# Twenty-eight float16 warm-up matmuls become three in float32 (linear attention followed by a silu MLP)

## The chip, the cores and the metric

The kernel runs on one core of one Trainium2 chip. The metric is the device time of one execution in microseconds. Five engines take part: TensorE (PE, with its weight loads listed apart as PEld), VectorE (DVE), ScalarE (ACT), GpSimd (POOL) and SyncE (SP), the last of which only issues DMA transfers here.

## The reference

For each of 8 batches and 8 heads, with 576 rows and 64 columns, the kernel computes an attention without a score matrix, and runs its result through a two-layer MLP:

```python
q_s = softmax(q, axis=-1)            # over the 64 columns
k_s = softmax(k, axis=2)             # over the 576 rows
kv  = einsum('bhsd,bhse->bhde', k_s, v)
x   = einsum('bhsd,bhde->bhse', q_s, kv)   # heads side by side: 4608 x 512
h   = x @ w_in                       # 512 x 2048
out = (h * sigmoid(h)) @ w_out       # 2048 x 512, float32
```

The warm-up matmuls compute nothing of this. They multiply a tile of zeros, and what they write to PSUM is overwritten before anything reads it.

## The kernel before

The order of all work is written out by hand. `ORDER` is a long list of names. Each name stands for a closure in `ops`, and the last loop of the kernel calls them in that order. Every engine works through its own instructions in that order; semaphores hold an instruction until what it reads is there. Nothing is moved by a planner, so taking a name out of the list moves nothing else.

The head of the list treats batch 0 alone, and it is this part that the change touches:

- SP loads q, k and v of batch 0 in two halves (`lq0.*`, `lk0.*`, `lv0.*`, line 152). A half `c` has four heads. Meanwhile DVE clears the tile `warm` (line 546) and converts the identity matrix (line 559), and TensorE starts on `heat0`.
- For each half: ACT takes exp(q) (`eq0.*`, line 163), DVE sums it and takes the reciprocal (`z0.*`, lines 207 to 211) and scales (`n0.*`, line 216), TensorE transposes the scaled q into PSUM (`tr0.*`, line 234, nine blocks of 128 columns), and ACT and DVE copy the transposes to SBUF (`tc0.*`, lines 142 and 144).
- For each half, beside that: ACT takes exp(k) (`ek0.*`, line 168), v is cast (`vc0.*`, on ACT for half 0, on ACT and DVE for half 1), TensorE forms kv with a column of ones for the softmax sum (`kv0.*`, line 248, 36 small matmuls of 64 by 64 by 65), and DVE divides by that sum (`kc0.*`, lines 259 and 261).
- Then `X0.*` (line 282) multiplies the transposed q by kv, and ACT and DVE bring the product to SBUF (`x0.*`).
- After `X0.1` the wide first layer of batch 0 begins (`w0.0`, `w2.0` and so on, line 307): 128 matmuls of 288 columns. From there on the list gives TensorE one matrix product after another until the end: the second layer, and for the later token tiles two layers of products by a Strassen-like scheme (lines 425 and 503).

The weights come by DMAs issued from POOL in four pieces of `w_in` (`W1a0` and `W1a1`, `W1b`, `W1c`, `W1d`, line 567), then pieces of `w_out` (line 573). The piece `W1b` holds the weights from the fifth block of the first layer on.

Four groups of warm-up matmuls stand in this head, all from line 564 and each 128 by 128 by 512 in float16:

- `heat0`, 20 of them into PSUM bank 5, ahead of the first transposes `tr0.0`
- `heat1`, 5 into bank 5, between `tr0.0` and `kv0.0`
- `heat2`, 1 into bank 6, between `X0.0` and `kv0.1`
- `heat3`, 2 into bank 3, between `kv0.1` and `X0.1`

Their operand `warm` is a view of `XS4[0]`, a float16 tile that is used for something else only much later.

Of the kernel before, what the change touches and what calls it, by code (L numbers as in the profile page):

```python
# [8 lines left out]
FP32 = mybir.dt.float32  # L9
# [7 lines left out]

ORDER = """
    lq0.0 lq0.1 lk0.0 lv0.0 lk0.1 lv0.1 gate W1a0 W1a1 W1b W1c W1d heat0 eq0.0.0 z0.0.0 eq0.0.1 z0.0.1 eq0.1 lq1.0
    lq1.1 W2a n0.0 ek0.0 z0.1 tr0.0 vc0.0 heat1 n0.1 tc0.0b kv0.0 tc0.0a kc0.0 tr0.1 ek0.1 vc0.1b X0.0 heat2 tc0.1b  # L20
    vc0.1a kv0.1 kc0.1 tc0.1a x0.0v heat3 X0.1 x0.0a x0.1v w0.0 w2.0 w1.0 x0.1a W2b1 lk1.0 w1.1 h1 w0.1 w3.0 w2.1
    W2b2 w3.1 h0 v1 v0 w5.0 w5.1 w4.0 w4.1 h2 v2 h3 w6.0 w6.1 h5 v3 h4 v5 w7.0 w7.1 h7 WS1.1 w9.0 v4 h6 w9.1 WS0.1
    w8.0 w8.1 v7 lk1.1 h9 h8 w11.0 v6 eq1.0.0 w11.1 v9 v8 h11 WS1.2 w10.0 lv1.1 w10.1 v11 w12.0 w12.1 eq1.0.1 W2c1
    h10 w13.0 lv1.0 v10 w13.1 w15.0 h12 h13 qp1a w15.1 v12 qp1b h15 v13 w14.0 eq1.1.0 z1.0 w14.1 eq1.1.1 p0 WS0.3 p1
# [46 lines left out]
def kernel(  # L71
# [9 lines left out]
    nc = tc.nc  # L81
# [9 lines left out]
    TCH = 512  # L91
# [15 lines left out]
    mp = ctx.enter_context(tc.tile_pool(name="mp", bufs=2))  # L107
# [10 lines left out]
    XS4 = [glob.tile([128, 2, HT], FP16, name=f"XS{i + 1}") for i in range(4)]  # L118
# [7 lines left out]
    dummy = glob.tile([1, 1], FP32, name="dummy")  # L126
    PS = ps.tile([128, 8, 512], FP32, name="PS")

    warm = XS4[0].rearrange("p a n -> p (a n)")
    B11, B12 = W2[:, 0:HF, 0:HN], W2[:, 0:HF, HN:DM]  # L130
    B21, B22 = W2[:, HF:NFB, 0:HN], W2[:, HF:NFB, HN:DM]
    T3 = B12
# [426 lines left out]
    nc.vector.tensor_copy(ident, ident_f)  # L559
    nc.vector.memset(vaug[:, :, :, D:E1], 1.0 / XS)  # L560

    def heat(n, bank=5):
        for _ in range(n):
            nc.tensor.matmul(out=PS[:, bank, :], lhsT=warm[:, 0:128], rhs=warm, start=True, stop=True)

    def load_w1(f0, f1, c0=0, c1=NC):
        nc.gpsimd.dma_start(
# [17 lines left out]
    def op(name, f, *args):  # L585
        assert name not in ops
        ops[name] = lambda: f(*args)
# [30 lines left out]
    for c, b0, b1 in ((0, 4, 0), (1, 6, 2)):  # L618
        op(f"X0.{c}", lambda c=c, b0=b0, b1=b1: (xt_mm(0, c, 0, 320, b0, 0), xt_mm(0, c, 320, 256, b1, 0)))
        op(f"x0.{c}a", xt_evac, 0, c, b0, 0, 320, 0, nc.scalar)  # L620
        op(f"x0.{c}v", xt_evac, 0, c, b1, 0, 256, 320, nc.vector)
    for i, (n, bank) in enumerate(((20, 5), (5, 5), (1, 6), (2, 3))):
        op(f"heat{i}", heat, n, bank)
    op("gate", lambda: nc.gpsimd.tensor_copy(gate, st[0]["kt", 0][0:1, 1, 0:1]))
    for x, f, n, c0, c1 in (("W1a0", 0, 4, 0, 2), ("W1a1", 0, 4, 2, 4), ("W1b", 4, 4, 0, 4), ("W1c", 8, 4, 0, 4), ("W1d", 12, 4, 0, 4)):
        op(x, load_w1, f, f + n, c0, c1)
# [38 lines left out]
    for b in range(1, B):  # L665
# [10 lines left out]
        if b > 1:  # L676
            bank = 2 if b in KV_WITH_X.values() else 6
# [16 lines left out]
    for t in range(1, NCH):  # L694
# [6 lines left out]
        for g in range(2):  # L701
            n = f"{t}.{g}."
# [123 lines left out]
```

## Time and profile before

| | us |
|---|---|
| median of three runs | 256.94 |
| lowest and highest of them | 256.66, 257.74 |
| the profiled execution, its own time | 256.38 |
| its span, from the first to the last instruction | 254.6 |
| TensorE busy in the span | 248.8 |
| VectorE busy | 207.0 |
| ScalarE busy | 190.7 |
| GpSimd busy | 66.0 |

All numbers of an execution's inside come from the profiled one. It lies 0.56 us under the median, and 1.8 us of its time lie outside the span. Times on the timeline count from the span's start. A row of the timeline gives the start, the length, the engine, the line, the operation, what is written and read, its size, how many instructions are merged into the row, and in brackets how long the engine had been idle and what ended that. A matmul's record lasts until its result is out, so the records of successive matmuls overlap: the pace of a row of them is read from the starts, not from the length of one.

### The profile page before, as it was taken

The numbers are of one execution on the slowest core, as the hardware profiler recorded it, in microseconds if no ns is written. First come the engines' busy times: TensorE is split into PE (matmuls) and PEld (weight loads), VectorE is DVE, ScalarE is ACT, GpSimd is POOL, SyncE is SP. The second block draws the span as 40 slices with busy tenths as digits, with TensorE's granted clock in tenths as the row PEclk, the third lists the DMA queues.
The fourth block names the chain that finished last, engine by engine and source line by source line (L and its number), as shares of the span: only waits on it lengthen the run. The fifth ranks groups of instructions, "written<-read, shape, count | busy, mean of one in ns | idle before, by whom it ended". The sixth has DMA issues, their size and how long they took to land.

```text
span 254.6 us, 6459 instructions
## 1 busy us (share of the span) xinstructions
PE 248.8 (98%) x2728; PEld 204.3 (80%) x2728; DVE 207.0 (81%) x277; ACT 190.7 (75%) x226; POOL 66.0 (26%) x62
## 2 busy tenths in 40 slices
PE   8899999999999999999999999999999999999994
PEld 2467746667888888888888888888888888888883
DVE  2969998899999989997998986996569836886752
ACT  4866867899999999999879889736597656674311
POOL 1753872730451540530082050006000000000022
PEclk9999999999999999999999999999999999999999
DMA  6999999799949939995955950030807000700355
GB/s 251 345 205 299 282 333 330 292 168 391 401 104 270 401 114 225 350 297 145 324 215 103 216 213 0 3 75 10 175 3 165 3 1 3 158 9 0 71 137 125
DMA packets 36238, 45.90 MB, mean 180 GB/s; under 512 B 16481, under 2 KB 21281, under 8 KB 36209
## 3 DMA queue, kind: packets, MB, share of 16 engines
q1 hardware_dynamic: 29408, 33.56, 45.4%
q0 software_dynamic: 6160, 11.60, 17.6%
q10 hardware_dynamic: 640, 0.33, 0.6%
q8 instruction: 21, 0.34, 0.5%
q14 instruction: 9, 0.07, 0.1%
HBM read 36.70 MB, written 9.44 MB: 181 GB/s over the span
## 4 chain that ended last, share of the span: by engine, by line
PE 81%; DMA 10%; ACT 3%; POOL 2%; DVE 2%; issue 1%; ACTq 0%
PE PS L503 37%; PE PS L425 34%; DMA qt<-in_q_dram 6%; PE PS L307 4%; DMA vt<-in_v_dram 3%; PE PS L335 2%; PE PS L282 2%; PE PS L248 2%; ACT eq L163 1%; DMA out_dram<-ow 1%; POOL eq L216 1%; POOL W L573 1%; DVE zq L207 1%; POOL h L181 1%; ACT sg L320 0%
## 5 line engine op out<-in xcount | busy, mean ns | idle before, releaser
L403 DVE TENSOR_TENSOR h<-PS,h 128x1024 f32<-128x1024 f32 (+1 forms) x45 | 54.1, 1204 | 8.7 <-PE PS L425 7.8
L503 PEld LDWEIGHTS <-GT 128*128 128x128 f16 x512 | 50.0, 98 | 6.0
L425 PEld LDWEIGHTS <-WS 128*128 128x128 f16 x480 | 46.6, 98 | 6.7 <-issue 0.8
L409 ACT ACTIVATE GT<-h 128x1024 f16<-128x1024 f32 (+1 forms) x45 | 46.7, 1050 | 0.9 <-DVE h L403 0.7
L503 PE MATMUL PS<-W,GT 128*128 128x256 f16 x384 | 47.2, 273 | 0.0
L425 PE MATMUL PS<-XS,WS 128*128 128x256 f16 (+1 forms) x360 | 45.0, 272 | 0.0
L142 ACT COPY h<-PS 128x1024 f32<-128x1024 f32 (+1 forms) x31 | 31.1, 1002 | 16.5 <-PE PS L425 14.6
L503 PEld LDWEIGHTS <-S 128*128 128x128 f16 x384 | 37.1, 98 | 4.7
L425 PEld LDWEIGHTS <-W 128*128 128x128 f16 x360 | 35.1, 98 | 4.5 <-issue 0.2
L216 POOL TENSOR_TENSOR eq<-eq,rzq 128x1152 bf16<-128x1152 bf16 x13 | 27.6, 2137 | 35.1 <-DVE rzq L211 35.0
L503 PE MATMUL PS<-T,S 128*128 128x256 f16 x256 | 32.0, 273 | 0.0
L144 POOL CAST vaug<-vt 128x1152 bf16<-128x1152 f32 x12 | 15.7, 1323 | 61.1 <-DMA vt<-in_v_dram 61.1
L425 PE MATMUL PS<-XT,W 128*128 128x256 f16 (+1 forms) x240 | 29.9, 272 | 0.0
L144 DVE COPY h<-PS 128x1024 f32<-128x1024 f32 (+1 forms) x14 | 17.0, 1211 | 8.4 <-PE PS L425 3.5
L163 ACT ACTIVATE eq<-qt 128x1152 bf16<-128x1152 f32 (+1 forms) x19 | 18.8, 1007 | 4.6 <-DMA qt<-in_q_dram 4.3
L778 POOL DMA_DIRECT2D out_dram<-ow x5 | 2.7, 545 | 70.0 <-DVE ow L760 70.0
L168 ACT ACTIVATE ek<-kt 128x1152 bf16<-128x1152 f32 x16 | 18.5, 1161 | 3.1 <-DMA kt<-in_k_dram 3.1
L409 ACT ACTIVATE GT<-PS 128x1024 f16<-128x1024 f32 (+1 forms) x15 | 15.2, 1013 | 6.5 <-PE PS L425 6.5
L207 DVE TENSOR_REDUCE zq<-eq 128x18 f32<-128x1152 bf16 x13 | 17.5, 1346 | 1.0 <-ACT eq L163 0.7
L503 PE MATMUL PS<-T,GT 128*128 128x256 f16 x128 | 16.3, 273 | 0.0
L503 PE MATMUL PS<-W,S 128*128 128x256 f16 x128 | 16.1, 273 | 0.0
L307 PE MATMUL PS<-XT,W 128*128 128x288 f16 x128 | 15.9, 287 | 0.0
(85 smaller groups left out, 335.5 us busy)
## 6 DMA issues: line engine op xcount, KB each, us to landing
out_dram<-ow SPq DMA_DIRECT2D x64, 128.0 KB, 2.9
qt<-in_q_dram SPq DMA_DIRECT2D x12, 576.0 KB, 5.9
kt<-in_k_dram SPq DMA_DIRECT2D x12, 576.0 KB, 7.0
vt<-in_v_dram SPq DMA_DIRECT2D x12, 576.0 KB, 6.7
qt<-in_q_dram POOLq DMA_DIRECT2D x4, 576.0 KB, 12.1
kt<-in_k_dram POOLq DMA_DIRECT2D x4, 576.0 KB, 12.4
vt<-in_v_dram POOLq DMA_DIRECT2D x4, 576.0 KB, 11.7
W<-in_moe_w_in_dram POOLq DMA_DIRECT2D x3, 512.0 KB, 10.1
```

Of the source, the lines that this page charges most:

```text
L142: eng.copy(out=o, in_=i)
L144: eng.tensor_copy(o, i)
L163: nc.scalar.activation(out=half(st[b]["eq"], cc)[:, :, g0:g1], in_=jgd(b, "qt", cc)[:, :, g0:g1], func=ACT.Exp)
L168: nc.scalar.activation(out=half(ek, cc), in_=jgd(b, "kt", cc), func=ACT.Exp)
L207: nc.vector.reduce_sum(out=z, in_=e, axis=AX.X)
L216: eng.tensor_tensor(out=e, in0=e, in1=r[:, :, :, None].to_broadcast([128, J, 2, D]), op=ALU.mult)
L248: nc.tensor.matmul(out=PS[s * 64:(s + 1) * 64, bank + r, cc * 128:cc * 128 + E1], lhsT=ek[r * 64:(r + 1) * 64, j, (2 * cc + s) * D:(2 * cc ...
L307: nc.tensor.matmul(out=PS[:, WIDE[fb] + n, 0:S // 2], lhsT=W1[:, c, fb * 128:(fb + 1) * 128], rhs=XTS[0][:, c, n * (S // 2):(n + 1) * (S / ...
L403: nc.vector.tensor_tensor(out=four(t, i), in0=group_bank(t, g), in1=four(t, i), op=ALU.add)
L409: nc.scalar.activation(out=group_out(t, f, n), in_=x, func=ACT.Silu, scale=1.0 / XS)
L425: nc.tensor.matmul(out=PS[:, bank + p // 2, (p % 2) * HT:(p % 2) * HT + width(t)], lhsT=a[:, c, p * 128:(p + 1) * 128], rhs=bb[:, c, 0:wid ...
L503: nc.tensor.matmul(out=PS[:, bank, m * HN:(m + 1) * HN], lhsT=a[:, fc, m * 128:(m + 1) * 128], rhs=bb[:, fc, :], start=(first and fc == 0) ...
```

## The change

The four groups of warm-up matmuls become one. It stands where `heat0` stood, ahead of the first transposes, and has three matmuls. Its operand is the first half of the scratch tile `h2`, in float32, so each is 128 by 128 by 512 in float32, and the DVE memset that clears it covers 128 by 512 float32 elements in place of 128 by 512 float16. The names `heat1`, `heat2` and `heat3` leave the list. Float32 matmuls load their weights themselves: the instruction list has no separate weight load for them. On every other engine the order of instructions is as it was.

```diff
 ORDER = """
     lq0.0 lq0.1 lk0.0 lv0.0 lk0.1 lv0.1 gate W1a0 W1a1 W1b W1c W1d heat0 eq0.0.0 z0.0.0 eq0.0.1 z0.0.1 eq0.1 lq1.0
-    lq1.1 W2a n0.0 ek0.0 z0.1 tr0.0 vc0.0 heat1 n0.1 tc0.0b kv0.0 tc0.0a kc0.0 tr0.1 ek0.1 vc0.1b X0.0 heat2 tc0.1b
-    vc0.1a kv0.1 kc0.1 tc0.1a x0.0v heat3 X0.1 x0.0a x0.1v w0.0 w2.0 w1.0 x0.1a W2b1 lk1.0 w1.1 h1 w0.1 w3.0 w2.1
+    lq1.1 W2a n0.0 ek0.0 z0.1 tr0.0 vc0.0 n0.1 tc0.0b kv0.0 tc0.0a kc0.0 tr0.1 ek0.1 vc0.1b X0.0 tc0.1b
+    vc0.1a kv0.1 kc0.1 tc0.1a x0.0v X0.1 x0.0a x0.1v w0.0 w2.0 w1.0 x0.1a W2b1 lk1.0 w1.1 h1 w0.1 w3.0 w2.1
...
-    warm = XS4[0].rearrange("p a n -> p (a n)")
+    warm = mp.tile([128, 2 * TCH], FP32, name="h2", bufs=1)[:, 0:512]
...
-    def heat(n, bank=5):
+    def heat(n):
         for _ in range(n):
-            nc.tensor.matmul(out=PS[:, bank, :], lhsT=warm[:, 0:128], rhs=warm, start=True, stop=True)
+            nc.tensor.matmul(out=PS[:, 5, :], lhsT=warm[:, 0:128], rhs=warm, start=True, stop=True)
...
-    for i, (n, bank) in enumerate(((20, 5), (5, 5), (1, 6), (2, 3))):
-        op(f"heat{i}", heat, n, bank)
+    op("heat0", heat, 3)
```

## The prediction

> **What bounds the kernel now.** I read the page's engine table and chain first, then the waits of TensorE, then the timeline of the first 20 us, where all four warm-up groups stand, and last the equal stretches around the two places where TensorE's pace changes.
>
> ```profile
> span 254.6 us, 6459 instructions
> PE 248.8 (98%) x2728; PEld 204.3 (80%) x2728; DVE 207.0 (81%) x277; ACT 190.7 (75%) x226; POOL 66.0 (26%) x62
> ...
> PEclk9999999999999999999999999999999999999999
> ...
> PE 81%; DMA 10%; ACT 3%; POOL 2%; DVE 2%; issue 1%; ACTq 0%
> ```
>
> TensorE is busy for 248.8 of 254.6 us and holds 81% of the chain that ended last. The row of the granted clock has a 9 everywhere, in the first slice too; the timeline below shows half pace there, so that row can't be used for this question, and I go by the pace of the matmuls.
>
> The waits of TensorE, in total and their number:
>
> ```profile
> PE PS L564 <- DVE XS L546: 1.2, 1, 1.2
> PE PS L234 <- DVE eq L216: 0.5, 1, 0.5
> ```
>
> There are two: the 1.2 us until the warm-up tile is cleared, and 0.5 us before the second transposes. From the start of the wide layer to the last product TensorE has one matmul after the other. So what starts the wide layer later, or runs part of it slower, is not made good behind it, and what the head loses is read at one place: where the wide layer's products stand on TensorE.
>
> The head, first the long warm-up:
>
> ```profile
> 0.89 0.27 DVE L546 MEMSET XS<- 128x256 uint32 x1
> ...
> 1.22 7.33 PE L564 MATMUL PS<-XS 128*128 128x512 f16 x20 [1.22 <-DVE XS L546]
> 1.34 0.23 DVE L559 CAST ident<-h 128x128 bf16<-128x128 f32 x1 [0.17 <-POOL h masks.py:199]
> ...
> 2.05 0.15 PEld L564 LDWEIGHTS <-XS 128*128 128x128 f16 x1 [0.28 <-issue]
> ...
> 5.21 1.41 DVE L209 TENSOR_REDUCE zq<-eq 128x9 f32<-128x576 bf16 x2 [3.48 <-ACT eq L163]
> ...
> 6.32 0.15 PEld L564 LDWEIGHTS <-XS 128*128 128x128 f16 x1 [0.28 <-issue]
> ...
> 6.75 0.15 PEld L564 LDWEIGHTS <-XS 128*128 128x128 f16 x1 [0.28 <-issue]
> ...
> 6.96 1.36 DVE L216 TENSOR_TENSOR eq<-eq,rzq 128x1152 bf16<-128x1152 bf16 x1
> 7.10 0.96 PEld L564 LDWEIGHTS <-XS 128*128 128x128 f16 x5 [0.20 <-issue]
> ...
> 8.47 0.66 PE L234 MATMUL PS<-ident,eq 128*128 128x128 bf16 x9
> ```
>
> The weight loads of the warm-up come one per matmul, so their starts give the pace. From 2.05 to 6.32, ten steps, it is 0.427 us. The five merged at 7.10 take 0.96 us together, some 0.21 a step. So TensorE went from half pace to full pace at about 7.0 us (the load before, at 6.75, still has a long record), 5.8 us after the first matmul and 1.4 us before the first transposes at 8.47, which wait for the scaled q (DVE, 6.96 + 1.36 = 8.32).
>
> Then the sparse part, up to the wide layer:
>
> ```profile
> 8.96 1.24 PE L564 MATMUL PS<-XS 128*128 128x512 f16 x5
> 9.12 1.16 ACT L142 CAST vaug<-vt 128x1152 bf16<-128x1152 f32 x1 [0.34 <-DMA vt<-in_v_dram]
> ...
> 10.34 0.48 PE L248 MATMUL PS<-vaug,ek 64*64 64x65 bf16 x36
> ...
> 11.34 0.68 PE L234 MATMUL PS<-ident,eq 128*128 128x128 bf16 x9 [0.52 <-DVE eq L216]
> ...
> 12.07 0.44 PE L282 MATMUL PS<-qT,kvn 64*64 64x320 bf16 x8
> 12.12 0.68 ACT L142 CAST vaug<-vt 128x576 bf16<-128x576 f32 x1 [0.19 <-DMA vt<-in_v_dram]
> ...
> 12.44 0.39 PE L564 MATMUL PS<-XS 128*128 128x512 f16 x1
> 12.70 0.68 ACT L142 COPY qT<-PS 128x640 bf16<-128x640 bf16 x1
> ...
> 12.85 0.56 PE L248 MATMUL PS<-vaug,ek 64*64 64x65 bf16 x36
> ...
> 13.34 0.60 PE L564 MATMUL PS<-XS 128*128 128x512 f16 x2
> ...
> 13.66 0.29 DVE L261 TENSOR_TENSOR kvn<-PS,rz 128x128 bf16<-128x128 f32 x1
> ...
> 14.01 0.44 PE L282 MATMUL PS<-qT,kvn 64*64 64x320 bf16 x8
> ...
> 14.38 15.89 PE L307 MATMUL PS<-XT,W 128*128 128x288 f16 x128
> ...
> 18.34 11.63 PEld L307 LDWEIGHTS <-W 128*128 128x128 f16 x96 [0.17 <-DMA W<-in_moe_w_in_dram]
> ...
> 249.01 1.91 PE L503 MATMUL PS<-T,GT 128*128 128x256 f16 x16
> ```
>
> ```profile
> 4.49 7.60 DMA vt<-in_v_dram
> ```
>
> The chain runs through the load of v, which lands at 12.09; then the cast on ACT (12.12 to 12.80), `kv0.1` on TensorE (12.85), the division on DVE (ends at 13.95), `X0.1` (14.01) and the wide layer (14.38). The warm-up groups lie beside it: `heat1` ends before the cast of v ends at 10.28, `heat2` lies under the cast, `heat3` under the division.
>
> **The change part by part.** *Work removed.* `heat1`, `heat2` and `heat3` take 1.24, 0.39 and 0.60 us of TensorE, all while the next real matmul waits for ACT or DVE. Taken alone, their removal gives nothing: their cover is idle time. `heat0` ends at 8.55 as its row says, 0.08 behind the first transposes' start; a free TensorE could start them at most 0.15 us sooner (8.32), and their result is copied by an ACT that is in the cast of v until 10.28. I take 0.
>
> *The memset.* 128x256 32-bit elements take 0.27 us, twice as many at most 0.54. The first matmul starts at 1.5 in place of 1.22, the identity's conversion (1.34) 0.1 us later; the next DVE work is at 5.21. I take 0, bounds 0 and 0.
>
> *Three float32 matmuls.* No row of before has one. If they go at the float16 pace, three take 3 x 0.427 = 1.28 us. If each is four products of half-width operands (an estimate: two halves by two halves), they take 12 x 0.427 = 5.1 us, and with a weight load of 0.15 exposed at each, 12 x 0.577 = 6.9 us. They would end at 2.8, 6.6 or 8.4 us, all before 8.47, so they delay no transposes. I take 5.1, since in the rows above the loads of 0.15 run inside the pace of 0.427. The Trainium skill, page "FP8 and Floating Point Precision", section "TensorE Precision Notes", says that true FP32 is four passes through the array; no run here shows it yet, and it would give the same 5.1.
>
> *The pace of what follows.* This is the term that counts. In the profiled execution 5.8 us of unbroken matmuls came before full pace. Three float32 matmuls give 5.1, then nothing until 8.47: 1.9 us of idle. So in that execution the transposes would start at half pace. Stretches of 3.41 us laid from 7.02, a length of my choice that divides the time between the two changes into 73 equal parts (the last row lies behind the span and shows a clock that falls at 256.19, 249.17 us after 7.02):
>
> ```profile
> 0.19:3.61 3.42, 2.39 (x6) 1.00 0.45 146
> 3.61:7.02 3.41, 3.41 (x9) 1.00 1.05 399
> ...
> 10.43:13.85 3.42, 2.83 (x92) 1.00 1.17 238
> 249.36:252.78 3.42, 1.56 (x15) 1.00 0.81 183
> 252.78:254.60 1.82, 0.00 (x0) 1.00 0.24 56
> 256.00:257.00 1.00, 0.00 (x0) 0.78 0.00 0
> ```
>
> The stretch that ended without a change was 70% busy (2.39 of 3.42), the one that ended with full pace 100%. At the other end 46% busy kept it, and an idle one lost it (the last product, at 249.01 above, ends at 250.92). Without the warm-ups the stretch from 10.43 to 13.85 has only its real work, and the one before has the transposes and `kv0.0`, 0.66 + 0.48 of 3.41 us, a third.
>
> At half pace the sparse part costs this. Lengths of one record, to take the pipeline out of the rows:
>
> ```profile
> L234 PE MATMUL PS<-ident,eq 128*128 128x128 bf16 x18 | 1.3, 220 | 0.5 <-DVE eq L216 0.5
> L248 PE MATMUL PS<-vaug,ek 64*64 64x65 bf16 x72 | 1.0, 194 | 0.1
> ```
>
> `tr0.1`: 0.68 less 0.22 is 0.46 of streaming, doubled it ends near 12.5; `X0.0` then runs up to 0.3 us later, which the cast hides, since `kv0.1` waits for 12.80. `kv0.1`: 0.56 less 0.19 is 0.37, at most 0.37 more. `X0.1`: its 320 and 256 columns at 0.21 us per 512 are 0.24, so 0.24 more. Together 0.5 us (bounds 0.25 if the small matmuls are held by their issue, and 1.7 if every TensorE row from 11.34 on doubles in full and none is hidden). The wide layer then starts at 14.9. At full pace it has 15.89 / 128 = 0.124 us a matmul; at half pace 0.24 (288/512 of 0.427), so each microsecond at half pace loses 0.5.
>
> When does full pace come? TensorE is nearly dense from 11.34 on at half pace. By the 5.8 us of the profiled execution it comes at 17.1; counted from 14.0, where nothing breaks the row any more, at 19.8. I take 17.1: 2.2 us at half pace, 1.1 lost. The wide layer's wait of 0.17 for the second piece of `w_in` at 18.34 is then gone. The sum: 0 + 0 + 0.5 + 1.1 - 0.17 = 1.4 to 1.5 us. On the profiled execution's 256.38 that is 257.9; the median lay 0.56 above it, so 258.4. The bounds: 0.25 - 0.17, with full pace just as the wide layer begins, gives 257.0; 0.5 + 2.4 - 0.17 gives 259.7; 1.7 + 1.85 - 0.17 gives 260.3. Past the head nothing changes: the rows of DVE, ACT, POOL and SP are in the same order, and the loads that POOL issues wait for ACT and the wide layer, so they shift along.
>
> **The rivals.** *Full pace is reached and kept (not slower).* Place: the stretch in which the float32 matmuls lie. It decides when a stretch that is busy enough fits into 1.5 to 6.6 us, and when a third of a stretch busy is enough to keep full pace until 14.4. For it: the share that is enough lies anywhere between 70% and 100%; in this execution's own phase the float32 matmuls would fill 3.0 of 3.41 us before 7.02, 87%; 46% kept the pace at the end. Against it: the 1.9 us of idle and a third busy, under the 46% seen. Its time: 0 from every term, 256.9, within 0.3.
>
> The Trainium skill, page "TensorE: Matmul & The Clock Gate", section "What's actually happening", has a free-running window of 3413 ns that doesn't begin with the kernel, and one busy window for full clock; the two changes here lie 249.17 us apart, 73 such windows, which agrees. By it 5.1 us of float32 hold a whole window in half of the phases, (5.1 - 3.41) / 3.41, and a nearly whole one in more, which is this rival; with none it is the forecast. The phase would differ from run to run.
>
> *Full pace comes in the sparse part, or is lost only late.* With full pace from 14.7 or so the cost is 0.5 - 0.17: 257.3. For it: the records fill 83% of 10.43 to 13.85 already at full pace, and more at half. Against it: that includes `heat2` and `heat3`.
>
> *The head gets shorter.* The most that the warm-ups could have held is 0.15 us at 8.32, off the chain; v lands at 12.09 either way. 256.8; for a gain of 1.3 no row speaks.
>
> *The change doesn't do what it says* can't be: the instruction list has three float32 matmuls and none of the others.
>
> **How the numbers follow.** About 0.5% (1.3 us) is what a measurement of this kernel can tell from no change: its three runs spread over 1.1. The forecast's case has 0.55; the rival that keeps full pace 0.33; the late one 0.09; a shorter head 0.03. I rate the forecast above its rival because both conditions of that must hold, and each is about even or somewhat better. Of the forecast's case one part in ten stays under 1.3 us. So slower 0.50, same 0.46, faster 0.04. The predicted time is the forecast's, 258.4, its own range 257.3 to 259.9. The whole range goes down to the rival's 256.4 and up to 260.1.
>
> **What would show it.** In the changed profile: float32 records at line 564 that end near 6.6; transposes with starts 0.11 apart at 8.47 in place of 0.055 (0.66 less 0.22, over eight steps); a row of `kv0.1` and `X0.1` that is longer; the wide layer from 14.9, its first weight loads 0.24 apart, then 0.12 from about 17.1; the last product 1.4 us later than 250.9. Wrong it is if the transposes and the wide layer run at full pace from the start, if float32 goes past 8.4 and holds the transposes, or if a late start of the wide layer is made good by shorter gaps behind.

## The result and the profile after

The changed kernel takes 258.92 us in the median of six runs (258.33 to 259.49), the kernel before 256.94 in six runs beside it. The ratio is 1.0074, with a 95% interval from 1.0054 to 1.0094: slower by 2.0 us. The forecast was 258.4 in a range from 256.4 to 260.1. The profiled execution took 258.99 us, 2.61 more than that of before, so it shows a little more than the median's loss.

The page of the changed kernel, the lines that answer to those shown of before:

```profile
span 257.2 us, 6415 instructions
...
PE 248.0 (96%) x2706; PEld 205.4 (80%) x2706; DVE 206.1 (80%) x277; ACT 191.4 (74%) x226; POOL 65.2 (25%) x62
...
PEclk9759999999999999999999999999999999999999
...
PE 92%; DVE 3%; DMA 2%; ACT 1%; issue 0%; ACTq 0%
```

TensorE is busy for 0.8 us less while the span is 2.6 us longer. The row of the granted clock now has a 7 and a 5 in its second and third slices: the clock's record has something to show here. The waits of TensorE:

```profile
PE PS L234 <- DVE eq L216: 2.1, 2, 1.9
PE PS L564 <- DVE h L546: 1.5, 1, 1.5
PE PS L248 <- ACT vaug L142: 1.3, 1, 1.3
PE PS L282 <- DVE kvn L261: 0.6, 1, 0.6
```

The idle time that the warm-ups filled is now visible: 1.9 us ahead of the first transposes, 1.3 ahead of `kv0.0`, 0.6 ahead of `X0.1`. The timeline of TensorE and of what it waits for:

```profile
0.94 0.48 DVE L546 MEMSET h<- 128x512 f32 x1
...
1.49 5.12 PE L564 MATMUL PS<-h 128*128 128x512 f32 x6 [1.49 <-DVE h L546]
...
8.51 0.66 PE L234 MATMUL PS<-ident,eq 128*128 128x128 bf16 x9 [1.91 <-DVE eq L216]
...
10.47 0.71 PE L248 MATMUL PS<-vaug,ek 64*64 64x65 bf16 x36 [1.30 <-ACT vaug L142]
...
11.38 1.14 PE L234 MATMUL PS<-ident,eq 128*128 128x128 bf16 x9 [0.19 <-DVE eq L216]
...
12.45 0.69 PE L282 MATMUL PS<-qT,kvn 64*64 64x320 bf16 x8
...
12.98 0.80 PE L248 MATMUL PS<-vaug,ek 64*64 64x65 bf16 x36
...
14.36 0.69 PE L282 MATMUL PS<-qT,kvn 64*64 64x320 bf16 x8 [0.59 <-DVE kvn L261]
...
14.99 18.17 PE L307 MATMUL PS<-XT,W 128*128 128x288 f16 x128
...
251.59 1.91 PE L503 MATMUL PS<-T,GT 128*128 128x256 f16 x16
```

The first transposes are the surprise: 0.66 us for nine, full pace, as before. From `kv0.0` on the rows are longer: 0.71 for 0.48, 1.14 for 0.68, 0.69 for 0.44. The wide layer starts 0.61 us later (14.99 for 14.38) and takes 2.28 us more (18.17 for 15.89). The stretches of 3.41 us, laid from the place where the clock's record begins, 6.10:

```profile
2.69:6.10 3.41, 3.41 (x6) 1.00 0.99 368
6.10:9.51 3.41, 1.16 (x11) 1.00 1.05 399
9.51:12.92 3.41, 2.26 (x53) 0.50 1.11 296
12.92:16.34 3.42, 2.83 (x56) 0.50 1.24 203
16.34:19.75 3.41, 3.41 (x16) 0.50 1.24 206
19.75:23.16 3.41, 3.41 (x29) 1.00 1.17 291
```

After length and TensorE's busy time the third last column is the granted clock. (The 1.00 of the first row says only that the record had not begun. The float32 matmuls there go at half pace: their records start 0.85 us apart, and in the kernel with six of them, below, that step falls to 0.43 where full pace comes.) TensorE came to full pace at 6.10, inside the float32 matmuls, lost it at 9.51, behind a stretch that was 34% busy, and had it back at 19.75. Between, 10.24 us at half pace. All six runs show the same granted share of the clock, 0.98, which is what half pace for 10.24 of 257.2 us makes (1 - 0.5 x 10.24 / 257.2).

The 2.89 us that TensorE is late behind the wide layer (0.61 + 2.28) become 2.58 at the last product (251.59 for 249.01). Of these 0.31 us, 0.24 are given back at one place, near 50 us (the first of the two TensorE rows below is 2.87 later than before, the second 2.63). The timeline of before there, a reduction on DVE and two rows of TensorE, then the same three of the changed kernel:

```profile
46.81 1.35 DVE L207 TENSOR_REDUCE zq<-eq 128x18 f32<-128x1152 bf16 x1 [0.75 <-ACT eq L163]
...
49.46 0.93 PE L425 MATMUL PS<-XS,WS 128*128 128x224 f16 x8
50.46 0.93 PE L425 MATMUL PS<-XS,W 128*128 128x224 f16 x8
```

```profile
48.86 1.34 DVE L207 TENSOR_REDUCE zq<-eq 128x18 f32<-128x1152 bf16 x1
...
52.33 0.93 PE L425 MATMUL PS<-XS,WS 128*128 128x224 f16 x8
53.09 0.93 PE L425 MATMUL PS<-XS,W 128*128 128x224 f16 x8
```

Before, the reduction waited 0.75 us for an exp, and TensorE's second row came 1.00 us after the first; in the changed kernel the reduction doesn't wait, and the step is 0.76. Work that DVE was late for was no longer late.

### The profile page after: what moved, and what is told of

Its sections match the earlier page's. It is cut to its first block, busy times and chain, and to the rows that moved or that the text cites. A ratio compares the mean times of both kernels' runs of the same rounds, so it can differ in the third digit from the quotient of the medians.

```text
span 257.2 us, 6415 instructions
## 1 busy us (share of the span) xinstructions
PE 248.0 (96%) x2706; PEld 205.4 (80%) x2706; DVE 206.1 (80%) x277; ACT 191.4 (74%) x226; POOL 65.2 (25%) x62
## 4 chain that ended last, share of the span: by engine, by line
PE 92%; DVE 3%; DMA 2%; ACT 1%; issue 0%; ACTq 0%
PE PS L503 37%; PE PS L425 35%; PE PS L307 7%; PE PS L445 5%; PE PS L335 2%; PE PS L282 2%; PE PS L248 2%; DMA qt<-in_q_dram 1%; DVE eq L216 1%; PE PS L234 1%; DMA out_dram<-ow 1%; DVE zq L209 1%; DVE zq L207 0%; DVE ow L759 0%; ACT ow L772 0%; ACT eq L163 0%
## 5 line engine op out<-in xcount | busy, mean ns | idle before, releaser
L425 PEld LDWEIGHTS <-W 128*128 128x128 f16 x360 | 35.2, 98 | 4.2
L144 POOL CAST vaug<-vt 128x1152 bf16<-128x1152 f32 x12 | 14.7, 1243 | 62.6 <-DMA vt<-in_v_dram 47.8
L307 PE MATMUL PS<-XT,W 128*128 128x288 f16 x128 | 18.2, 311 | 0.0
L307 PEld LDWEIGHTS <-W 128*128 128x128 f16 x128 | 13.5, 106 | 4.8 <-issue 0.4
```

The source lines that it names most:

```text
L144: eng.tensor_copy(o, i)
L307: nc.tensor.matmul(out=PS[:, WIDE[fb] + n, 0:S // 2], lhsT=W1[:, c, fb * 128:(fb + 1) * 128], rhs=XTS[0][:, c, n * (S // 2):(n + 1) * (S / ...
L425: nc.tensor.matmul(out=PS[:, bank + p // 2, (p % 2) * HT:(p % 2) * HT + width(t)], lhsT=a[:, c, p * 128:(p + 1) * 128], rhs=bb[:, c, 0:wid ...
```

## The experiments

Two theories stood at first. *Idle theory:* full pace is lost because the stretch behind the warm-up holds too little TensorE work; float16 or float32 makes no difference. *Type theory:* float32 wakes or holds the clock worse. A third, the *late-groups theory*, says that the eight later warm-ups alone hold the clock, however long the first group is. All kernels compute the whole reference; they differ in warm-ups alone, and in the clearing of their operand. "Share" below is TensorE's busy time in a stretch by the records. "Streaming" is the same with each record shortened by 0.175 us, about what a record is longer than the step to the next (at full pace 0.38 against 0.21 us for 512 columns, 0.29 against 0.12 for 288).

**Twelve float16 in front, none later** (from the kernel before):

```diff
-    for i, (n, bank) in enumerate(((20, 5), (5, 5), (1, 6), (2, 3))):
+    for i, (n, bank) in enumerate(((12, 5), (0, 5), (0, 6), (0, 3))):
```

> Twelve float16 warm-ups ahead of the first transposes (12 x 0.427 = 5.1 us, the length of the three float32 ones) and none later. Idle theory (full pace is lost because a stretch of 3.4 us behind the warm-up has only about a quarter of TensorE work; the type of the operand plays no part): as the changed kernel, 258.9 within 0.6, half pace from about 9.5 to about 19.7. Type theory (float32 warm-ups wake or hold the clock worse than float16): near the kernel before, 256.9 within 0.4.

Measured: 258.86 us (258.71 to 259.00, four runs), ratio 1.0082 [1.0060, 1.0105]. Its stretches:

```profile
5.60:9.01 3.41, 1.03 (x12) 1.00 1.05 395
9.01:12.43 3.42, 1.96 (x48) 0.50 1.11 329
12.43:15.84 3.41, 2.82 (x58) 0.50 1.19 194
15.84:19.25 3.41, 3.41 (x16) 0.50 1.24 207
```

The same course as with float32, and the same time. The type theory falls: twelve float16 matmuls (4.91 us here) and three float32 ones (5.12 us) are worth the same.

**No warm-up at all** (from the changed kernel):

```diff
-    op("heat0", heat, 3)
+    op("heat0", heat, 0)
```

> No warm-up matmul at all (their zero tile is still cleared). Idle theory: TensorE is at half pace from the start to about 16 to 20 us, as the changed kernel is from 9.5 to 19.8; only the first transposes differ, whose copy waits for ACT anyway: 258.9 within 0.7, so the three float32 matmuls bring nothing. If they do bring something, this is slower than the changed kernel by 0.5 or more.

Measured: 258.88 us (258.61 to 259.03, four runs), ratio 1.0082 [1.0062, 1.0101], and full pace first at 19.22. Its transposes take 1.12 us instead of 0.66:

```profile
8.49 1.12 PE L234 MATMUL PS<-ident,eq 128*128 128x128 bf16 x9 [8.49 <-DVE eq L216]
```

So the three float32 matmuls of the change bring nothing: the full pace that they gain is spent on idle time and on the first transposes, whose copy waits for ACT anyway.

**Three float32 in front, the eight later ones put back** (they are float16, on the old tile):

```diff
+    warm32 = mp.tile([128, 2 * TCH], FP32, name="h2", bufs=1)[:, 0:512]
...
+    nc.vector.memset(warm32, 0.0)
     nc.vector.memset(warm, 0.0)
...
-    def heat(n, bank=5):
+    def heat(n, bank=5, w=warm):
...
-            nc.tensor.matmul(out=PS[:, bank, :], lhsT=warm[:, 0:128], rhs=warm, start=True, stop=True)
+            nc.tensor.matmul(out=PS[:, bank, :], lhsT=w[:, 0:128], rhs=w, start=True, stop=True)
...
-    for i, (n, bank) in enumerate(((20, 5), (5, 5), (1, 6), (2, 3))):
-        op(f"heat{i}", heat, n, bank)
+    for i, (n, bank) in enumerate(((3, 5), (5, 5), (1, 6), (2, 3))):
+        op(f"heat{i}", heat, n, bank, warm if i else warm32)
```

> Three float32 warm-ups in front, and the eight later float16 ones put back. Idle theory: the gap of 2 us stays, but the stretch behind the float32 ones has the first half of the five later ones in it, about 40% busy, between the 34% (by the records) that lost the clock in the changed kernel and the 46% that kept it at the end of the kernel before: kept gives 256.9 to 257.3, lost gives half pace for at most two stretches, 258.0 within 0.6. Late-groups theory: 256.9. Type theory: 258.9.

Measured: 256.69 us (256.49 to 257.05, ten runs), ratio 1.0006 [0.9996, 1.0017]: the whole loss is gone.

```profile
6.48:9.90 3.42, 1.51 (x14) 1.00 1.05 396
9.90:13.31 3.41, 2.71 (x79) 1.00 1.16 283
13.31:16.72 3.41, 3.34 (x63) 1.00 1.20 190
```

In this profiled run the stretch behind the float32 matmuls is 44% busy and keeps full pace, though the idle gap ahead of the transposes is still 1.9 us long. Not every run kept it: four of the ten have a granted share of 0.991 to 0.993, about what one stretch at half pace makes (1 - 0.5 x 3.41 / 255), yet they took 256.65 to 256.85 us, no longer than the others. Where that stretch lay in them is not shown; the kernel with the five, below, has one that cost next to nothing. Replacing `heat0` alone costs nothing; the loss of the change comes from leaving out the eight.

**Twenty float16 in front, none later:**

```diff
-    for i, (n, bank) in enumerate(((20, 5), (5, 5), (1, 6), (2, 3))):
+    for i, (n, bank) in enumerate(((20, 5), (0, 5), (0, 6), (0, 3))):
```

> The 20 float16 warm-ups of before ahead of the first transposes, the eight later ones left out. Idle theory: the gap of 2 us is filled, the stretch behind 7.0 is some 58% busy and keeps full pace; the next, to 13.9, has 36% real work. If that is enough the time is 256.9 within 0.4; if not, half pace from about 13.9 to about 17.3, 258.3 within 0.5. Late-groups theory (it is the eight later ones alone that hold the clock): 258.9, with half pace from about 10.

Measured: 258.25 us in the median of ten runs, but spread: 256.32, 256.67, four from 258.05 to 258.29, four from 258.87 to 259.24; ratio 1.0059 [1.0033, 1.0084]. Its profile fell on the run of 256.32 and shows full pace throughout. None of the three expected values holds for all runs: runs near each of them occur. The late-groups theory falls with the run of 256.32, which kept full pace without any later group. The eight runs of 258.05 us or more have a granted share of 0.987, which two stretches at half pace make; what parts those near 258.2 from those near 259.0 is not shown. So the kernel was profiled twice more.

> The 20 float16 warm-ups in front alone once more, for a profile of another kind of run: its times were 256.3 to 256.7, 258.0 to 258.3 and 258.9 to 259.2. If the kinds differ by where the 3.4 us stretches lie, a run of 258 or more shows full pace until a boundary near 9 to 13 us, half pace for one to three stretches behind it, and a lost stretch that is less than 44% busy.

> As the run before it, a third profile of the same kernel, to see a second kind of run if the other shows the first again.

Measured: 256.34 and 258.84 us, one run each, and so one of each kind. The stretches of the run of 256.34 us, then of the run of 258.84:

```profile
6.86:10.27 3.41, 2.28 (x17) 1.00 1.05 394
10.27:13.68 3.41, 2.15 (x89) 1.00 1.17 267
```

```profile
5.53:8.95 3.42, 2.71 (x19) 1.00 1.03 390
8.95:12.36 3.41, 1.63 (x58) 1.00 1.10 337
12.36:15.77 3.41, 2.42 (x56) 0.50 1.22 192
15.77:19.19 3.42, 3.42 (x16) 0.50 1.24 206
```

The instructions are the same, the boundaries are not: 6.86 in one run, 5.53 in the other. In the second a stretch lies on the sparsest part, from 9.0 to 12.4, and ends with half pace for two stretches. What decides the cost is where the stretches happen to lie.

**Six float32 in front, none later** (from the changed kernel, `heat` called with 6):

> Six float32 warm-ups in front, none later: the idle between warm-up and first transposes is filled (they end near 8.9 if full pace comes at 6 to 7 us, and hold the transposes by up to 0.5, which their copy on ACT hides). Idle theory: like 20 float16 in front alone, so several kinds of runs between 256.5 and 259.2, median near 258.2. Type theory: 258.9 throughout.

Measured: 259.25 us (256.76 to 259.43, nine runs, seven of them at 258.79 or more), ratio 1.0073 [1.0045, 1.0101]. The median lies 0.35 us above the type theory's 258.9 and 1.05 above the idle theory's 258.2, so by the time alone the type theory does better. The profile shows why it isn't the type: full pace comes at 5.89 (the loads of the float32 matmuls start 0.85 us apart before it, 0.43 behind it), holds through the float32 matmuls and is lost in the sparse part.

```profile
5.89:9.30 3.41, 3.41 (x15) 1.00 1.06 399
9.30:12.72 3.42, 1.87 (x58) 1.00 1.13 313
12.72:16.13 3.41, 2.67 (x50) 0.50 1.23 202
```

The lost stretch is 55% busy by the records, more than the 44% that kept the pace above. Plain busy time does not order the cases. It is made of short matmuls, each with its tail in the record; streaming it is 30%.

**Three float32 and only the five behind the first transposes** (as the third experiment, with `(0, 6), (0, 3)` at the end):

> Three float32 warm-ups in front and only the five float16 ones behind the first transposes; the last three left out. Idle theory: the stretch that the changed kernel loses (34% busy by the records) is back at about 44%, which kept the clock with all eight later ones; the next stretches have 50% or more of real work and warm-up: 256.7 within 0.4, so the five alone carry the whole difference. Spread theory (every later group is needed, as the sparse part alone can lose the clock): two kinds of runs, 256.7 and about 258.3.

Measured: 257.10 us, nine runs from 256.82 to 257.97 and one of 259.68; ratio 1.0025 [1.0000, 1.0051]. The median is as the idle theory has it, the spread is not. Its profile fell on an early boundary:

```profile
1.16:4.57 3.41, 3.08 (x4) 1.00 0.75 254
4.58:7.99 3.41, 1.26 (x3) 1.00 1.02 379
7.99:11.40 3.41, 2.94 (x14) 0.50 1.05 394
11.40:14.81 3.41, 2.66 (x99) 1.00 1.17 184
```

Full pace at 4.58 behind a stretch that was 90% busy, lost at 7.99, and back at 11.40, since the transposes and the five warm-ups, at half pace, fill that stretch to 86%. This run took 256.87 us, the median of the kernel before beside it 256.85: a stretch at half pace that is over before the wide layer begins costs next to nothing. In seven of the ten runs the granted share is 0.990 to 0.993, about one stretch; the run of 259.68 has 0.987, two.

**The kernel before without its last three warm-ups, and without its five:**

```diff
-    for i, (n, bank) in enumerate(((20, 5), (5, 5), (1, 6), (2, 3))):
+    for i, (n, bank) in enumerate(((20, 5), (5, 5), (0, 6), (0, 3))):
```

```diff
-    for i, (n, bank) in enumerate(((20, 5), (5, 5), (1, 6), (2, 3))):
+    for i, (n, bank) in enumerate(((20, 5), (0, 5), (1, 6), (2, 3))):
```

> The kernel before without its last three warm-ups (20 in front, five behind the first transposes). Threshold theory (TensorE keeps full pace through a stretch of 3.41 us when more than about a third of it is streaming, by the records less 0.175 us of tail each; it lost it at 0.31 and less, kept it at 0.34 and more): the stretches that lost the clock with 20 alone lie from about 9 to 12.7 and get the five back, so nearly every run is 256.9 within 0.4, spread under 1.0. Spread theory (each later group is needed): runs of 258 and more among them.

> The kernel before without the five behind the first transposes (20 in front, one and two later). Threshold theory: the stretch from about 9 to 12.4 has no warm-up in it and loses the clock at 0.28 to 0.30 as with 20 alone, so runs of 258 and more among the times, median between 257 and 258.5. Spread theory the same; if all runs are at 256.9, it is the last three that hold the clock and the threshold is misread.

Measured: the first 257.16 us (256.46 to 258.37, ten runs), ratio 1.0018 [0.9996, 1.0040]; the second 258.17 us (256.49 to 259.40, ten runs), ratio 1.0043 [1.0017, 1.0070]. The second is as expected: the stretch without the five loses the clock.

```profile
9.19:12.61 3.42, 1.65 (x54) 1.00 1.09 312
12.61:16.02 3.41, 3.06 (x49) 0.50 1.16 184
```

The first missed: the median is right, but four of its ten runs lie at 257.8 to 258.4, where I had expected a spread under 1.0. These four have a granted share of 0.993, one stretch at half pace; the other six, the profiled one among them, have 0.999 or 1.00. I had looked only at stretches from about 9 to 12.7. By the records of the profiled run, a stretch that begins between 9.9 and 11.3 us would stream only 0.30 to 0.36, less than one from 9.0 (0.58) or 12.4 (0.45), so the five alone leave no margin there; that such a stretch was the lost one in the four runs is an estimate and not shown. In the profiled run of the kernel before, no stretch that begins behind 7.0 us streams less than 0.45 until the kernel's end, wherever it lies, and in that kernel's 56 runs beside the experiments the granted share is 0.997 or more. Their times go from 256.15 to 258.03 us all the same, and one run of the second kernel took 258.26 with a share of 1.00: a time alone doesn't say what the clock did.

Stretches at full pace that decide between the explanations, the sparsest ones of each kind among them:

| kernel | stretch | share | streaming | full pace behind it |
|---|---|---|---|---|
| changed | 6.10 to 9.51 | 0.34 | 0.21 | lost |
| twelve float16 | 5.60 to 9.01 | 0.30 | 0.22 | lost |
| twenty float16, the 258.84 us run | 8.95 to 12.36 | 0.48 | 0.28 | lost |
| six float32 | 9.30 to 12.72 | 0.55 | 0.30 | lost |
| before without its five | 9.19 to 12.61 | 0.48 | 0.31 | lost |
| three float32 and five | 4.58 to 7.99 | 0.37 | 0.31 | lost |
| three float32 and five, end of the kernel | 250.33 to 253.75 | 0.32 | 0.24 | lost |
| twenty float16, the 256.32 us run, end of the kernel | 249.41 to 252.82 | 0.43 | 0.34 | kept |
| three float32 and eight | 6.48 to 9.90 | 0.44 | 0.35 | kept |
| twenty float16, the 256.32 us run | 10.48 to 13.89 | 0.62 | 0.35 | kept |
| twenty float16, the 256.34 us run | 10.27 to 13.68 | 0.63 | 0.36 | kept |
| before, end of the kernel | 249.36 to 252.78 | 0.46 | 0.37 | kept |
| before | 10.43 to 13.85 | 0.83 | 0.52 | kept |

By streaming the two kinds part between 0.31 and 0.34; by share they overlap. The longest idle gap doesn't order them either: it is 0.79 us in the lost stretch of the six float32 and 1.91 in the kept one of the three float32 and eight. That the limit is near a third is read from these rows and was not set by a run of its own, and it moves with the tail that is taken off: with 0.165 us in place of 0.175 the kinds part between 0.35 and 0.38, with 0.18 they touch. Toward full pace: stretches at half pace with 0.86, 0.91 and 1.00 streaming brought it, those with 0.73 or 0.74 in four kernels did not.

## Why the prediction was right, and where not

*The direction and the size* were right: 258.4 forecast, 258.92 measured. The place was right too: the wide layer at half pace, nothing made good behind it but 0.3 us. Two things in it are luck. The sum on the profiled execution was 1.5 us where 2.6 were measured; the 0.56 added for the median hid half of that, since the changed kernel's profiled execution lies at its median and not under it. And the course of events was another than forecast (told below), at the same price: the kernel without any warm-up, which never reaches full pace in the head, took 258.88 us.

*The work removed, the memset, no delay of the transposes:* as forecast. The memset took 0.48 us (at most 0.54 forecast), the first float32 matmul started at 1.49, the transposes at 8.51. They start 0.04 later than before, as the exp of q does.

*Three float32 matmuls take 5.1 us:* 5.12 measured, in six records of 512 columns at 0.85 us each. The profile lists a weight load for every record, 0.33 us from the third on and inside that step, though the instruction list has no separate one. The four passes that the Trainium skill's page "FP8 and Floating Point Precision", section "TensorE Precision Notes", gives agree with that length: 12 x 0.427.

*"So in that execution the transposes would start at half pace":* this step failed. I had taken the 5.8 us of warm-up ahead of full pace as what is needed. It is not; 4.6 us sufficed in the changed kernel (1.49 to 6.10), and 3.1 in the kernel with the early boundary (1.49 to 4.58). What was needed is one stretch of 3.41 us that is nearly full (0.86 of it sufficed in one run, 0.74 did not), and how long that takes depends on where the boundaries lie: the stretch before 4.58 was 90% busy, the one before 6.10 wholly. The first condition of the rival held; its second, that a third of a stretch is enough to keep full pace, is what failed. The order of events was: reached, then lost. My second rival had the loss as late and cheap, 257.3; it came at 9.51 and cost as much as having no warm-up.

The Trainium skill's page "TensorE: Matmul & The Clock Gate", section "What's actually happening", with its free-running window of 3413 ns, fits all of this: every change of the clock in every profile here lies a whole number of such windows from the next (in the changed kernel 1, 3 and 70 of them), and with a warm-up in front the first one fell at 4.58 to 7.06 us of the span, differently from run to run. Its condition for half clock, an idle window, is too weak: the windows that lost it in the head were 21 to 31% streaming.

*The sparse part costs 0.5 us:* the wide layer started 0.61 later, of which up to 0.13 may be the load of v, which came later by that in this execution (the cast starts at 12.25 for 12.12). Right.

*Full pace at 17.1, so 1.1 us lost in the wide layer, less a wait of 0.17:* mis-sized, both terms. Full pace came at 19.75; the first 20 steps of the wide layer took about 0.24 us each in place of 0.12, and the layer took 2.28 us more, where the forecast had 0.9. The wait for weights before was worth less than its 0.17: it is a wait of the weight loads, and the starts of the matmuls there are 0.153 and 0.134 us apart in place of 0.123, 0.04 in all. I had taken the work from 11.34 on as nearly dense. The stretch from 12.92 to 16.34 was 83% busy and 73% streaming, with 0.59 us idle ahead of `X0.1`, and that does not bring full pace; only the next did, which lies wholly in the wide layer. My other end, 19.8, was the right one.

*Past the head nothing changes:* nearly. 0.3 us came back near 50 us, where TensorE had waited for DVE.

## What to carry to other kernels

A warm-up is worth only what it is joined to. Three float32 matmuls brought TensorE to full pace and then let it idle for 1.9 us, and the kernel ran as if they were not there; the few matmuls scattered in the waits behind them, which lie on no chain and whose removal frees nothing, were worth the whole 2 us. With the three float32 ones in front, putting them back brought the time to that of the kernel before; with twenty float16 in front and without them, eight of ten runs were 258.05 us or more. Where real work is sparse, sum what TensorE streams in every stretch of 3.4 us, tails of the records left out, for every place the stretches may have, and fill those near or under a third, above all those that end where the dense work begins.

Judge such a kernel by many runs. With 20 warm-ups in front and none later the same program ran in 256.3 or 259.2 us, and one profile of a run of 256.3 would have made the later ones look useless.

## What the runs showed that was not expected

The return to full pace is harder than the keeping of it: a stretch that streams 0.34 keeps it, 0.74 does not bring it back. That gap is why a loss at 9.5 us lasted until 19.75, three stretches, with TensorE more than 80% busy in the second.

The transposes seem to count. The kept stretch of the third experiment streams 0.35, of which 0.11 are transposes; without them it would stand at 0.24, under the lost 0.31 of a stretch that holds none. The Trainium skill's page "TensorE: Matmul & The Clock Gate", section "Part 4: PE-mode transpose", says that a transpose does not count as busy in the same way; these two rows speak against that here, though the shares are worked out from records and no run varied the transposes alone.
